# Column norms of two weight matrices: the four blocks of squares are added on VectorE before TensorE sums over partitions

## The chip, the core and the metric

The kernel runs on one core of a Trainium2 chip. The metric is the device time of one execution in microseconds (us); lower is better. A core has five engines that run side by side, each through its own list of instructions in order: TensorE (PE: matrix products, with PEld for the loading of the stationary operand), VectorE (DVE), ScalarE (ACT), GpSimd (POOL) and SyncE (SP, which here only starts DMAs). They wait for one another by semaphores. An instruction that waits holds up all that stands behind it on its engine.

## What is computed

An attention over a small memory of 32 slots per head, followed by a two-layer network on its output. Cut to what matters:

```
a = softmax of phi over the 576 positions
k_m, v_m = a^T k, a^T v                       # 32 x 64 per head
attn = softmax(q k_m^T / 8)
x = attn v_m                                  # 4608 tokens x 512
h = x @ w_in                                  # w_in 512 x 2048
out = (h - tanh(h)) @ w_out                   # w_out 2048 x 512
```

The kernel has a quick path that is exact enough only while the numbers stay within bounds (h small, weights neither tiny nor large). So it also computes, beside the main work, the sums of squares of the weights' columns and compares them with a lower and an upper bound. Should a comparison fail, a second, slower path (`wide_path`) runs after the first.

## The kernel before

The weights are split into a high and a low float16 part, `win_hi` and `win_lo`, `wout_hi` and `wout_lo`. The tokens go in 18 units `u` of 256, and each unit in four blocks `fb` of 512 hidden features. After a start whose order is written out by hand, a loop walks over *slots*, one `(u, fb)` each, numbered from 18; a slot takes about 8 us. Every engine then follows the order in which the program emits instructions (`in_order`), and no scheduler moves anything.

One slot emits, in this order:

- `mm1`: 24 or more matrix products of TensorE into the tile `hs` (L534), and ScalarE's square of `hs` (L541);
- `g1`, VectorE (L549), and then the words of the first part of the slot's plan;
- ScalarE's second square (L554); `a_forms`, four float16 sums or differences of VectorE into `f` (L581); and `g2`, VectorE (L558);
- `mm2_blocks`: the second product for a slot further back, L660 and L667 on TensorE;
- the words of the second part of the plan (behind `;`);
- `g2_high`, ScalarE (L563), and `g3`, GpSimd (L568);
- late steps, such as the squares of the weights (`SI`, `SO`) and GpSimd's pass over reloaded weights (`CW`, tile `fy`, L408); then `evict`, which on the last block of a unit sends the finished output through VectorE (L716 to L727);
- the words of the third part (behind `|`); after that the next slot's `mm1`.

The squares: `squares_in(fb)` takes 512 columns of `win_hi` in four blocks of 128 rows and leaves `sqi`, a tile of 128 partitions x (4 x 512) float16; `squares_out(part)` does the same for `wout_hi` into `sqo`. One slot later `norms_in` and `norms_out` sum them over the partitions. For each group of 128 columns TensorE loads a 128x128 block of squares as its stationary operand and multiplies it by a column of ones; the four blocks are accumulated in PSUM. That is 16 pairs of load and product in each of eight places, the slots 32, 40, 48, 55, 57, 59, 61 and 63 (`NI0` to `NI3`, `NO0` to `NO3`). They stand between a slot's `mm2_blocks` and the next slot's `mm1`. ScalarE copies the four resulting columns out (L428, L445).

Of the kernel before, what the change touches and what calls it, by code (L numbers as in the profile page):

```python
# [14 lines left out]
ALU = mybir.AluOpType  # L15
# [3 lines left out]
P = 128  # L19
# [20 lines left out]
CW = (  # L40
    0.33333331252017, -0.13333128520786, 0.053934788850892, -0.021660115374759,
    0.0082189218977914, -0.0025104593252184, 0.000420695493864,
)
# [1 line left out]


V_WIN = (2.0 ** -12, 0.0025)
WI_WIN = (2.0 ** -6, 1.5)
WO_WIN = (2.0 ** -6, 3.5)
N_F1 = 32  # L50


# [254 lines left out]
def split_path(ctx, tc, c, ins, out):  # L307
    nc = tc.nc
# [53 lines left out]
    def conv(p):  # L362

        ts = [big.tile([P, 512], U32, tag=W_TAG[p], name=f"wt{p}{i}") for i in range(2)]
        yield from to_f32(p, ts)
        yield
        tfs[p] = [t.bitcast(F32) for t in ts]
        his[p] = half_of(p, win_hi, wout_hi)
        for i in range(2):
            nc.scalar.activation(his[p][:, i], tfs[p][i], AF.Copy, scale=S_W)  # L370
# [9 lines left out]
    def low(p):  # L380
        lo = low_of(p)
        for i in range(2):
            nc.vector.scalar_tensor_tensor(
                lo[:, i], tfs[p][i], S_W, his[p][:, i], op0=ALU.mult, op1=ALU.subtract
            )

    def low_pe(p):
        lo = low_of(p)
        pw = ps_h.tile([P, 2, 512], F32, tag="h", name=f"pw{p}")
        for i in range(2):  # L390
            nc.tensor.matmul(pw[:, i], c["idw"], tfs[p][i], start=True, stop=False)
            nc.tensor.matmul(pw[:, i], c["nid16"], his[p][:, i], start=False, stop=True)
        yield
        nc.scalar.activation(lo, pw, AF.Copy)

    def low_pool(p):
        lo = low_of(p)
        for i in range(2):
            nc.scalar.activation(tfs[p][i], tfs[p][i], AF.Copy, scale=S_W)
        yield  # L400
        for i in range(2):
            nc.gpsimd.tensor_tensor(lo[:, i], tfs[p][i], his[p][:, i], op=ALU.subtract)
# [11 lines left out]
    def squares_in(fb):  # L414
        acc["q", fb] = big.tile([P, 4, 512], F16, tag="q" if fb < 3 else "e", name=f"sqi{fb}", bufs=2 if fb < 3 else 1)
        nc.scalar.activation(acc["q", fb], win_hi[:, :, 512 * fb : 512 * fb + 512], AF.Square, scale=S_Q)

    def norms_in(fb):
        sq = acc.pop(("q", fb))
        pa = ps_a.tile([P, 2, 512], F32, tag="pa", name=f"pni{fb}")  # L420
        for k in range(4):
            for pr in range(4):
                nc.tensor.matmul(
                    pa[:, 0, k : k + 1], sq[:, pr, P * k : P * k + P], c["ones16"],
                    start=(pr == 0), stop=(pr == 3),
                )
        o = N_F1 + 2 * B + 4 * fb
        nc.scalar.activation(stat[:, o : o + 4], pa[:, 0, 0:4], AF.Copy, scale=(S_W * S_Q) ** -2)  # L428

# [4 lines left out]
    def norms_out(part):  # L434
        if part == 0:
            acc["n"] = big.tile([P, 4, 4], F32, tag="wn", name="wn", bufs=1)
        sq = acc.pop(("q", part))
        pa = ps_a.tile([P, 2, 512], F32, tag="pa", name=f"pno{part}")
        for k in range(4):
            for i in range(4):  # L440
                nc.tensor.matmul(
                    pa[:, 0, k : k + 1], sq[:, i, P * k : P * k + P], c["ones16"],
                    start=(i == 0), stop=(i == 3),
                )
        nc.scalar.activation(acc["n"][:, :, part], pa[:, 0, 0:4], AF.Copy, scale=(S_W * S_Q) ** -2)  # L445
        if part == 3:
            o = N_CHECK - 4
            nc.vector.tensor_reduce(stat[:, o : o + 4], acc["n"], axis=AX.X, op=ALU.add)
# [146 lines left out]
    acc = {}  # L595
# [149 lines left out]
    def two(f, g, *x):  # L745
# [15 lines left out]
        "AT": lambda b, t: att.soft_turn(b, st[b], t), "AS": lambda b, t: att_split(b, t, nc.gpsimd), "ASv": lambda b, t: att_split(b, t, nc.vector),  # L761
        "Z": warm, "P": att_p, "PL": att_pl, "H": mm1, "a": lambda u, fb: two(g1, g1_square, u, fb), "b": lambda u, fb: two(g2, g2_high, u, fb), "c": lambda u, fb: g3(u, fb, nc.gpsimd), "cv": lambda u, fb: g3(u, fb, nc.vector), "PLp": att_pl_pe,
        "T": lambda x, y: conv(10 * x + y), "L": lambda x, y: low_pool(10 * x + y), "Lv": lambda x, y: low(10 * x + y), "Lp": lambda x, y: low_pe(10 * x + y),
        "G": b_form, "SI": squares_in, "NI": norms_in, "SO": squares_out, "NO": norms_out,
        "GG": lambda: check(tc, c, big), "GX": lambda: check_all(tc, c, ps_a),
        "M": lambda u, fb: mm2(u, fb, fb in (0, 2), fb in (1, 3)), "R": load_part, "OP": save_part, "O": save,
    }
# [15 lines left out]
    for word in START.split():  # L783
        if ":" in word:
            k, tag = word.split(":")
# [15 lines left out]
    )  # L801

    PLAN_C = (
# [5 lines left out]
    )  # L809
    tasks = {}  # L810
# [82 lines left out]
def check(tc, c, big):  # L893
    nc = tc.nc
    stat = c["stat"]
    good = big.tile([P, N_CHECK], F32, tag="good", name="good", bufs=1)
    nc.vector.tensor_scalar(good[:, 0:N_F1], stat[:, 0:N_F1], 0.0, None, op0=ALU.is_le)
    o = N_F1
    for n, (lo, hi) in ((2 * B, V_WIN), (DF // P, WI_WIN), (DM // P, WO_WIN)):
        s, g = stat[:, o : o + n], good[:, o : o + n]  # L900
        nc.vector.tensor_scalar(g, s, lo, None, op0=ALU.is_ge)
        nc.vector.scalar_tensor_tensor(g, s, hi, g, op0=ALU.is_le, op1=ALU.mult)
        o += n
    row = big.tile([P, 1], F32, tag="grow", name="grow", bufs=1)
    nc.vector.tensor_reduce(row, good, axis=AX.X, op=ALU.add)
    c["row"] = row


def check_all(tc, c, ps_a):
    nc = tc.nc  # L910
    pa = ps_a.tile([P, 2, 512], F32, tag="pa", name="pgood")
    nc.tensor.matmul(pa[:, 0, 0:1], c["ones"], c["row"], start=True, stop=True)
    nc.vector.tensor_scalar(c["bad"], pa[:, 0, 0:1], P * N_CHECK - 0.5, None, op0=ALU.is_lt)
# [120 lines left out]
@with_exitstack  # L1034
def tile_kernel(ctx: ExitStack, tc: tile.TileContext, qt, kva, kvt, pha, phx, w_in, w_out, out):
    nc = tc.nc
    ins = dict(qt=qt, kva=kva, kvt=kvt, pha=pha, phx=phx, w_in=w_in, w_out=w_out)
    const = ctx.enter_context(tc.tile_pool(name="const", bufs=1))
    c = {}
    for name, shape, dt in (  # L1040
        ("ident", [P, P], F32), ("ones", [P, P], F32), ("ones16", [P, 1], F16), ("one", [P, 1], F32),
        ("beta", [P, 1], F32), ("idw", [P, P], F32), ("nidp", [P, P], F16), ("idw", [P, P], F32), ("nid16", [P, P], F16), ("stat", [P, N_CHECK], F32), ("bad", [P, 1], I32),
    ):
        c[name] = const.tile(shape, dt, name=name)
    make_identity(nc, c["ident"])
    nc.vector.tensor_scalar(c["nid16"], c["ident"], -1.0, None, op0=ALU.mult)
    nc.vector.tensor_scalar(c["nidp"], c["ident"], -S_V * S_W / S_P, None, op0=ALU.mult)
    nc.vector.tensor_scalar(c["idw"], c["ident"], S_W, None, op0=ALU.mult)
    nc.gpsimd.memset(c["ones"], 1.0)
    nc.gpsimd.memset(c["ones16"], 1.0)  # L1050
    nc.gpsimd.memset(c["one"], 1.0)
    nc.gpsimd.memset(c["beta"], BETA)
    with ExitStack() as inner:
        split_path(inner, tc, c, ins, out)
    bad = nc.values_load(c["bad"][0:1, 0:1], min_val=0, max_val=1)
    with tc.If(bad > 0):
        with ExitStack() as inner:
            wide_path(inner, tc, c, ins, out)
# [39 lines left out]
```

## Time and profile before

| | |
|---|---|
| runs shown | 678.45, 680.75 and 677.93 us; median 678.45 us |
| the profiled execution | 678.71 us, of which 676.9 us are the span of the profile |
| mean granted TensorE clock | 0.986 of full speed |
| HBM traffic | 73.55 MB read, 11.53 MB written |

A line of the timeline gives the start in us from the span's start, the duration in us, the engine, the line of the program, the operation, what is written and read, and its shape; `x16` means that 16 such instructions were merged. What stands in square brackets is the idle time of the engine ahead of the instruction, and what ended it. A line on the instructions of one tile or one source line gives smallest, median and largest duration in ns instead.

### The profile page before, as it was taken

The numbers are of one execution on the slowest core, as the hardware profiler recorded it, in microseconds if no ns is written. First come the engines' busy times: TensorE is split into PE (matmuls) and PEld (weight loads), VectorE is DVE, ScalarE is ACT, GpSimd is POOL, SyncE is SP. The second block draws the span as 40 slices with busy tenths as digits, with TensorE's granted clock in tenths as the row PEclk, the third lists the DMA queues.
The fourth block names the chain that finished last, engine by engine and source line by source line (L and its number), as shares of the span: only waits on it lengthen the run. The fifth ranks groups of instructions, "written<-read, shape, count | busy, mean of one in ns | idle before, by whom it ended". The sixth has DMA issues, their size and how long they took to land.

```text
span 676.9 us, 15461 instructions
## 1 busy us (share of the span) xinstructions
PE 645.2 (95%) x6628; PEld 449.3 (66%) x6628; DVE 512.3 (76%) x799; ACT 376.0 (56%) x506; POOL 256.7 (38%) x170
## 2 busy tenths in 40 slices
PE   4678989999999999999999999999999999999996
PEld 1335465565646567787777777777777777887874
DVE  4599899989655677966697868886888586867573
ACT  2458477765543356554566455646555587766541
POOL 0032623423211334452345344534453555455521
PEclk9878999999999999999999999999999999999999
DMA  8679653422312142125331523152415233234201
GB/s 346 248 270 386 242 172 128 177 99 80 125 64 90 54 148 72 63 52 188 92 112 45 191 73 128 48 192 68 133 49 183 68 103 126 72 120 132 84 32 37
DMA packets 26428, 86.16 MB, mean 127 GB/s; under 512 B 2928, under 2 KB 3184, under 8 KB 25584
## 3 DMA queue, kind: packets, MB, share of 16 engines
q1 hardware_dynamic: 25056, 82.87, 35.5%
q10 hardware_dynamic: 1296, 2.23, 0.9%
q8 instruction: 54, 0.88, 0.5%
q14 instruction: 22, 0.18, 0.1%
HBM read 73.55 MB, written 11.53 MB: 126 GB/s over the span
## 4 chain that ended last, share of the span: by engine, by line
PE 69%; DVE 6%; ACT 1%; DMA 1%; issue 0%; SPq 0%; DVEq 0%; ACTq 0%
PE hs L534 19%; PE o L660 12%; PE x L667 12%; PE o L667 9%; PE o L611 7%; PE h L534 2%; PE pp L486 2%; PE pkv L196 2%; DVE f L581 2%; PE o1h L611 2%; DVE h L549 1%; DVE h L558 1%; PE psc L240 1%; DMA kv<-in_kva_dram 1%; ACT u L541 1%
## 5 line engine op out<-in xcount | busy, mean ns | idle before, releaser
L568 POOL TENSOR_TENSOR g<-h,g 128x1024 f16<-128x1024 f32 x64 | 145.2, 2269 | 322.1 <-ACT g L563 212.3
L534 PEld LDWEIGHTS <-ph 128*128 128x128 f16 x2304 | 177.5, 98 | 22.4 <-issue 6.4
L534 PE MATMUL hs<-ah,ph 128*128 128x256 f16 (+3 forms) x1088 | 145.8, 248 | 0.0
L549 DVE SCALAR_TENSOR_TENSOR h<-hs,u 128x1024 f32<-128x1024 f32 x52 | 63.5, 1221 | 97.0 <-ACT u L541 93.8
L563 ACT ACTIVATE g<-h 128x1024 f16<-128x1024 f32 x72 | 76.0, 1055 | 94.8 <-DVE h L558 86.0
L534 PE MATMUL hs<-al,ph 128*128 128x256 f16 (+3 forms) x544 | 122.1, 248 | 0.0
L554 ACT ACTIVATE u<-u,beta 128x1024 f32<-128x1024 f32 x72 | 82.6, 1148 | 62.6 <-DVE h L549 62.1
L660 PE MATMUL o<-wout_hi,g 128*128 128x512 f16 x416 | 100.6, 380 | 1.5 <-DVE r L727 1.5
L558 DVE SCALAR_TENSOR_TENSOR h<-u,h 128x1024 f32<-128x1024 f32 x72 | 88.9, 1234 | 5.0 <-ACT u L554 4.6
L667 PEld LDWEIGHTS <-f 128*128 128x128 f16 x832 | 81.4, 98 | 9.5
L611 PEld LDWEIGHTS <-g 128*128 128x128 f16 x480 | 45.8, 98 | 59.0 <-issue 4.5
L541 ACT ACTIVATE u<-hs 128x1024 f32<-128x1024 f32 x52 | 53.0, 1020 | 52.5 <-PE hs L534 52.4
L611 PE MATMUL o<-wout_hi,g 128*128 128x512 f16 x256 | 78.5, 379 | 1.1 <-ACT g L563 0.6
L667 PE MATMUL x<-bt,f 128*128 128x256 f16 x624 | 76.6, 273 | 0.0
L667 PEld LDWEIGHTS <-g 128*128 128x128 f16 x624 | 60.6, 98 | 21.6 <-issue 0.8
L660 PEld LDWEIGHTS <-g 128*128 128x128 f16 x416 | 38.5, 98 | 48.4 <-issue 13.4
L581 DVE TENSOR_TENSOR f<-g 128x512 f16<-128x512 f16 x104 | 58.3, 600 | 3.4 <-POOL g L568 3.4
L534 PE MATMUL h<-ah,ph 128*128 128x256 f16 (+2 forms) x448 | 57.1, 245 | 0.0
L534 PE MATMUL h<-al,ph 128*128 128x256 f16 (+2 forms) x224 | 48.6, 245 | 0.6 <-DVE al L477 0.6
L611 PE MATMUL o<-wout_lo,g 128*128 128x512 f16 x128 | 48.5, 379 | 0.0
L504 DVE SCALAR_TENSOR_TENSOR ph<-pp,ph 128x1024 f16<-128x1024 f32 x30 | 36.4, 1213 | 1.9 <-ACT ph L499 1.7
L499 ACT ACTIVATE ph<-pp 128x1024 f16<-128x1024 f32 x32 | 32.5, 1016 | 4.3 <-PE pp L486 4.3
(137 smaller groups left out, 954.4 us busy)
## 6 DMA issues: line engine op xcount, KB each, us to landing
kv<-in_kva_dram SPq DMA_DIRECT2D x20, 516.0 KB, 4.0
q<-in_qt_dram SPq DMA_DIRECT2D x16, 576.0 KB, 4.1
chk<-in_w_in_dram SPq DMA_DIRECT2D x16, 512.0 KB, 5.1
chk<-in_w_out_dram SPq DMA_DIRECT2D x16, 512.0 KB, 3.5
out_dram<-r SPq DMA_DIRECT2D x25, 256.0 KB, 2.5
kv<-in_kva_dram SPq DMA_DIRECT2D x6, 1032.0 KB, 9.7
raws<-in_w_in_dram SPq DMA_DIRECT2D x12, 512.0 KB, 6.0
raw<-in_w_out_dram SPq DMA_DIRECT2D x12, 512.0 KB, 6.2
```

Of the source, the lines that this page charges most:

```text
L504: nc.vector.scalar_tensor_tensor(pl, pa, S_P / (S_V * S_W), ph, op0=ALU.mult, op1=ALU.subtract)
L534: nc.tensor.matmul(hp[:, k, tu : tu + w], px[:, g, cs], d[ax][:, g, ta : ta + w], start=(n == 0), stop=(n == 5),)
L541: nc.scalar.activation(uu, hp, AF.Square, scale=1.0 / (S_A * S_P))
L549: nc.vector.scalar_tensor_tensor(h3, hp, C2 * S_G / (S_A * S_P), uu, op0=ALU.mult, op1=ALU.mult)
L554: nc.scalar.activation(uu, uu, AF.Square, bias=c["beta"])
L558: nc.vector.scalar_tensor_tensor(h3, uu, CC, h3, op0=ALU.add, op1=ALU.mult)
L563: nc.scalar.activation(gg[:, 0], h3, AF.Copy)
L568: eng.tensor_tensor(gg[:, 1], h3, gg[:, 0], op=ALU.subtract)
L581: nc.vector.tensor_tensor(o, x, y, op=op)
L611: nc.tensor.matmul(o, gx[:, k, P * tt : P * tt + P], wx[:, 4 * fb + k, :], start=(first and k == 0 and wx is wout_hi and gx is gh), stop=( ...
L660: nc.tensor.matmul(o[th], gg[:, 0, k, P * th : P * th + P], wout_hi[:, 4 * fb + k, :], start=(first and k == 0), stop=False)
L667: nc.tensor.matmul(dst, a(1 - n, kk), b(n, kk), start=(new and kk == 0 and n == 0), stop=(end and kk == 1 and n == 1))
```

## The change

VectorE adds the four blocks of squares in place, in two steps: blocks 0 and 1 plus blocks 2 and 3 (128x1024), then block 0 plus block 1 (128x512). TensorE then makes one pair of load and product for each group of 128 columns, 4 in place of 16. The new step, `SS`, stands in the second part of the plan of the same slot as the norms. The bounds of the comparison are drawn in by 0.2% for the rounding of the added float16 sums.

```
-WI_WIN = (2.0 ** -6, 1.5)
-WO_WIN = (2.0 ** -6, 3.5)
+WI_WIN = (1.002 * 2.0 ** -6, 1.497)
+WO_WIN = (1.002 * 2.0 ** -6, 3.493)
...
+    def squares_sum(i):
+        sq = acc["q", i]
+        nc.vector.tensor_tensor(sq[:, 0:2], sq[:, 0:2], sq[:, 2:4], op=ALU.add)
+        nc.vector.tensor_tensor(sq[:, 0], sq[:, 0], sq[:, 1], op=ALU.add)
...
         for k in range(4):
-            for pr in range(4):
-                nc.tensor.matmul(
-                    pa[:, 0, k : k + 1], sq[:, pr, P * k : P * k + P], c["ones16"],
-                    start=(pr == 0), stop=(pr == 3),
-                )
+            nc.tensor.matmul(pa[:, 0, k : k + 1], sq[:, 0, P * k : P * k + P], c["ones16"], start=True, stop=True)
...
-    (31, "CW CE SI0"), (32, "CW CW | NI0"),
+    (31, "CW CE SI0"), (32, "CW CW ; SS0 | NI0"),
...
-    (56, "CW CW CQ CQ SO0"), (57, "CW CW CQ CQ | NO0"),
+    (56, "CW CW CQ CQ SO0"), (57, "CW CW CQ CQ ; SS0 | NO0"),
```

`norms_out` is changed as `norms_in` is, and the other six places of the plan get `SS` in the same way.

Where the new instructions stand on their engines is shown at two places. The first is slot 32. This is VectorE there before the change: `f` are the sums of `a_forms`, `h` is `g2`, `sz` belongs to the attention's second softmax, and the next `h` is `g1` of slot 33.

```order
L581 TENSOR_TENSOR f_4010<-g_3958,f_4010 128x2x256
L558 SCALAR_TENSOR_TENSOR h_3996<-u_3994,h_3996 128x1024
L280 TENSOR_REDUCE sz_4061<-sc_3910 128x18
L281 TENSOR_SCALAR sz_4061<-sz_4061 128x18
L282 RECIPROCAL sz_4061<-sz_4061 128x18
L549 SCALAR_TENSOR_TENSOR h_4110<-hs,u_4108 128x1024
```

And this is VectorE at the same place now (lines below the edit are two less).

```order
L579 TENSOR_TENSOR f_4010<-g_3958,f_4010 128x2x256
L556 SCALAR_TENSOR_TENSOR h_3996<-u_3994,h_3996 128x1024
L421 TENSOR_TENSOR sqi_3965<-sqi_3965 128x1024
L422 TENSOR_TENSOR sqi_3965<-sqi_3965 128x512
L280 TENSOR_REDUCE sz_4063<-sc_3910 128x18
L281 TENSOR_SCALAR sz_4063<-sz_4063 128x18
L282 RECIPROCAL sz_4063<-sz_4063 128x18
L547 SCALAR_TENSOR_TENSOR h_4100<-hs,u_4098 128x1024
```

The two sums stand right behind `g2` (L556), ahead of the attention's work. On TensorE the place of the norms is unchanged, behind the last product of `mm2_blocks` (`f` as stationary operand) and ahead of the next slot's `mm1` (`hs`). So it stands there now, with the semaphores that are waited for:

```order
L665 LDWEIGHTS f_3916
L665 MATMUL o_3813<-wout_lo,f_3916 128x256
L428 LDWEIGHTS sqi_3965 [waits DVE_49,Activation_49]
L428 MATMUL pni_4068<-ones_60,sqi_3965 128x1 [waits PE_49]
L428 LDWEIGHTS sqi_3965
L428 MATMUL pni_4068<-ones_60,sqi_3965 128x1
L428 LDWEIGHTS sqi_3965
L428 MATMUL pni_4068<-ones_60,sqi_3965 128x1
L428 LDWEIGHTS sqi_3965
L428 MATMUL pni_4068<-ones_60,sqi_3965 128x1
L532 LDWEIGHTS ph_2992
L532 MATMUL hs<-ah_3041,ph_2992 128x256
```

Before, 16 such pairs (L423) stood in the place of these four. The first load now has to wait for VectorE's second sum; the `mm1` of the next slot (`hs`, L532) stands behind it.

The second place is slot 57, the last block of a unit, where the output leaves through VectorE. Before, the rows `r` of `evict` followed `g2` at once:

```order
L558 SCALAR_TENSOR_TENSOR h_7052<-u_7050,h_7052 128x1024
L716 SCALAR_TENSOR_TENSOR r_7061<-x,r_7061 128x256
L717 SCALAR_TENSOR_TENSOR r_7062<-x,r_7061 128x256
L718 TENSOR_TENSOR r_7061<-r_7061,r_7062 128x256
L719 TENSOR_TENSOR r_7062<-r_7062 128x256
L727 SCALAR_TENSOR_TENSOR r_7061<-o_6717,r_7061 128x512
```

Now the two sums stand between them:

```order
L556 SCALAR_TENSOR_TENSOR h_7012<-u_7010,h_7012 128x1024
L421 TENSOR_TENSOR sqo_6979<-sqo_6979 128x1024
L422 TENSOR_TENSOR sqo_6979<-sqo_6979 128x512
L714 SCALAR_TENSOR_TENSOR r_7021<-x,r_7021 128x256
L715 SCALAR_TENSOR_TENSOR r_7022<-x,r_7021 128x256
L716 TENSOR_TENSOR r_7021<-r_7021,r_7022 128x256
L717 TENSOR_TENSOR r_7022<-r_7022 128x256
L725 SCALAR_TENSOR_TENSOR r_7021<-o_6687,r_7021 128x512
```

All of `evict` has moved behind the sums; the same holds in slot 61. ScalarE, GpSimd and SyncE keep their order everywhere.

More of the change, by code (lines that the diff above doesn't have):

```diff
@@ L439, in norms_out @@
         for k in range(4):
[L440 to L444, printed above, removed]
+            nc.tensor.matmul(pa[:, 0, k : k + 1], sq[:, 0, P * k : P * k + P], c["ones16"], start=True, stop=True)
         nc.scalar.activation(acc["n"][:, :, part], pa[:, 0, 0:4], AF.Copy, scale=(S_W * S_Q) ** -2)
@@ L763, in split_path @@
         "T": lambda x, y: conv(10 * x + y), "L": lambda x, y: low_pool(10 * x + y), "Lv": lambda x, y: low(10 * x + y), "Lp": lambda x, y: low_pe(10 * x + y),
-        "G": b_form, "SI": squares_in, "NI": norms_in, "SO": squares_out, "NO": norms_out,
+        "G": b_form, "SI": squares_in, "NI": norms_in, "SO": squares_out, "NO": norms_out, "SS": squares_sum,
         "GG": lambda: check(tc, c, big), "GX": lambda: check_all(tc, c, ps_a),
```

8 rows, old and new, of the table PLAN_C are left out of this document.

## The prediction

> **What bounds the kernel now.** I read the page's busy shares and its chain first, then who TensorE waits for in the second half of the span, and last the timeline around the eight places where the norms are summed.
>
> ```profile
> PE 645.2 (95%) x6628; PEld 449.3 (66%) x6628; DVE 512.3 (76%) x799; ACT 376.0 (56%) x506; POOL 256.7 (38%) x170
> ...
> PE 69%; DVE 6%; ACT 1%; DMA 1%; issue 0%; SPq 0%; DVEq 0%; ACTq 0%
> ```
>
> The chain that ended last is TensorE's by 69% of the span. All eight places lie after 320 us; among TensorE's waits from 320 to 660 us the largest group is this (us in total, times, longest):
>
> ```profile
> PE o L660 <- DVE r L727: 1.5, 4, 1.0
> ```
>
> So in that stretch TensorE hardly ever waits, and a us taken from or added to its own list moves the end by a us. VectorE, busy 76% of the span, has room on average. But an average doesn't say when it has room, so the question is what VectorE is doing when TensorE arrives at the norms. This is the first place (slot 32), in the timeline:
>
> ```profile
> 334.52 1.22 DVE L558 SCALAR_TENSOR_TENSOR h<-u,h 128x1024 f32<-128x1024 f32 x1
> ...
> 335.07 0.56 PEld L423 LDWEIGHTS <-sqi 128*128 128x128 f16 x16
> 335.18 0.54 PE L423 MATMUL pni<-ones,sqi 128*128 128x1 f16 x16
> ...
> 335.58 0.27 PE L534 MATMUL hs<-ah,ph 128*128 128x256 f16 x1
> 335.66 0.74 DVE L280 TENSOR_REDUCE sz<-sc 128x18 f32<-128x576 f32 x1
> 335.77 1.06 ACT L563 ACTIVATE g<-h 128x1024 f16<-128x1024 f32 x1 [0.90 <-DVE h L558]
> ```
>
> TensorE arrives at 335.07, while VectorE is still in `g2` (L558, from 334.52). In the changed order the sums stand behind `g2`. TensorE will get there first.
>
> **What is removed.** The 16 pairs start at 335.18 and the next slot's `mm1` at 335.58: 0.40 us for 16, 25 ns a pair, although the duration shown for one product is 163 ns or so; products overlap. Twelve pairs fewer are 0.30 us per place, and 8 x 0.30 = 2.40 us in all. That is the whole gain there can be, 0.35%. The rows lie on TensorE's own list, so it is a real gain, if nothing waits.
>
> **What is added: two sums on VectorE.** No row has a 128x1024 sum of float16. The nearest are these:
>
> ```profile
> L581 DVE TENSOR_TENSOR f<-g x104: 379/417/1621, 240.9 to 665.5; 128x512 f16<-128x512 f16 x104
> ```
>
> ```profile
> L718 DVE TENSOR_TENSOR r<-r,r x13: 412/415/417, 277.4 to 669.7; 128x256 f32<-128x256 f32 x13
> ```
>
> The small sum (128x512) has its own row: 0.42 us. For the large one the floor is the same 0.42, the ceiling twice that, 0.84. A sum of 512 float16 takes as long as one of 256 float32, so an element costs half as much. A float32 pass of 1024 takes 1.22 us (L558) and one of 512 takes 0.64 (L727 below, 1.28 for two): 0.58 for 512 more, so 0.29 for 512 more of float16, and 0.42 + 0.29 = 0.71 us. I take 0.71.
>
> The next VectorE instruction starts 1.14 us after `g2` does (335.66 - 334.52). ScalarE, which waits for `g2`, starts 0.03 after its end (335.77 against 335.74); I take 0.03 for each hand-over. The second sum is then done, and TensorE let go, at the start of `g2` + 1.14 + 0.71 + 0.03 + 0.42 + 0.03 = **+2.33 us**. GpSimd could disturb this only if it were at work then; its `g3` waits for L563, which ends at 1.25 + 1.06 = 2.31 after that start, so the sums just escape it.
>
> **What TensorE waits.** At the first place 334.52 + 2.33 = 336.85 against 335.07: 1.78 us. Here are the others; the second is like the first and the third, so the third stands for both.
>
> ```profile
> 472.68 1.22 DVE L558 SCALAR_TENSOR_TENSOR h<-u,h 128x1024 f32<-128x1024 f32 x1
> 473.23 0.56 PEld L423 LDWEIGHTS <-sqi 128*128 128x128 f16 x16
> ...
> 533.60 1.22 DVE L558 SCALAR_TENSOR_TENSOR h<-u,h 128x1024 f32<-128x1024 f32 x1
> ...
> 535.04 0.56 PEld L423 LDWEIGHTS <-sqi 128*128 128x128 f16 x16
> ...
> 551.00 0.56 PEld L441 LDWEIGHTS <-sqo 128*128 128x128 f16 x16
> ...
> 551.67 1.22 DVE L558 SCALAR_TENSOR_TENSOR h<-u,h 128x1024 f32<-128x1024 f32 x1
> ...
> 567.96 0.56 PEld L441 LDWEIGHTS <-sqo 128*128 128x128 f16 x16
> ...
> 568.82 1.22 DVE L558 SCALAR_TENSOR_TENSOR h<-u,h 128x1024 f32<-128x1024 f32 x1
> ...
> 584.17 0.56 PEld L441 LDWEIGHTS <-sqo 128*128 128x128 f16 x16
> ...
> 584.85 1.22 DVE L558 SCALAR_TENSOR_TENSOR h<-u,h 128x1024 f32<-128x1024 f32 x1
> ...
> 600.38 0.56 PEld L441 LDWEIGHTS <-sqo 128*128 128x128 f16 x16
> ...
> 600.70 1.22 DVE L558 SCALAR_TENSOR_TENSOR h<-u,h 128x1024 f32<-128x1024 f32 x1
> ```
>
> From the fifth place on TensorE arrives before `g2` has even begun. By the same arithmetic (start of L558 + 2.33 - arrival) the eight waits are 1.78, 1.78, 1.78, 0.89, 3.00, 3.19, 3.01 and 2.65, together **18.1 us**. Less the 2.4 us of removed pairs, that is **+15.7 us**.
>
> What is queued behind: the whole `mm1` of the next slot, and with it that slot's chain (square on ScalarE, `g1`, second square, `g2`, `g3`). All of it hangs on `mm1` and is late by the same amount, so `g2` is no nearer to TensorE's arrival at the next place: the waits add up. Nothing later takes them up, as TensorE's own list has next to no idle time there (the 1.5 us row). The loads on SyncE's queue keep their order and get more time.
>
> **A second wait behind the first.** In slots 57 and 61 `evict` now stands behind the sums. These are the rows of slot 57:
>
> ```profile
> 547.35 2.04 POOL L408 TENSOR_TENSOR fy<-chk 128x512 f32<-128x512 f32 x2
> ...
> 549.01 1.95 DVE L581 TENSOR_TENSOR f<-g 128x512 f16<-128x512 f16 x2
> ...
> 549.34 1.34 POOL L284 TENSOR_TENSOR sc<-sc,sz 128x576 f32<-128x576 f32 x1
> ...
> 553.60 0.41 DVE L718 TENSOR_TENSOR r<-r,r 128x256 f32<-128x256 f32 x1
> ...
> 554.06 2.29 POOL L568 TENSOR_TENSOR g<-h,g 128x1024 f16<-128x1024 f32 x1 [3.38 <-ACT wn L445]
> ...
> 554.27 1.28 DVE L727 SCALAR_TENSOR_TENSOR r<-o,r 128x512 f32<-128x512 f32 x2
> ...
> 555.00 1.89 PE L660 MATMUL o<-wout_hi,g 128*128 128x512 f16 x8
> ...
> 556.32 2.03 POOL L408 TENSOR_TENSOR fy<-chk 128x512 f32<-128x512 f32 x2
> ```
>
> Two `f` sums that meet GpSimd take 1.95 us where two alone take some 0.8: they end at 550.96, 0.28 after GpSimd's L284, so each seems to wait out one GpSimd instruction. Today L718 and L719 are nearly through when GpSimd's `g3` starts at 554.06. With `evict` about 1.09 us later (0.74 for the first sum and its hand-over, 0.35 for the second), L718 comes at 554.69, in the middle of `g3`, which needs until some 556.2. If L718 waits for that, and L719 for the `fy` pass behind it (1.02 us), L719 ends near 557.9 and the first L727 at 558.55. TensorE, 2.70 us late by then (3.00 - 0.30), comes to L660 at 557.70 and needs the buffer `o` that L727 frees: 0.85 us more. If L719 slips in ahead of `fy`, it is 0. I take 0.85, as the `f` rows show one wait for each, and the same for slot 61: **+1.7 us**.
>
> **Sum.** 15.7 + 1.7 = 17.4 us on the profiled execution's 678.71 us (the median of the runs shown is 0.26 lower): **696.0 us**, 2.6% slower.
>
> **Rivals.**
>
> *The clock falls in the long waits.* The trace shows that the granted clock drops to half after pauses of TensorE:
>
> ```profile
> 28.59 1.09 PE L196 MATMUL pkv<-kv,e 128*32 128x129 f32 x32 [3.02 <-ACT e L180]
> ...
> 62.08 0.66 PE L225 MATMUL ptr<-ident,kvn 128*64 128x128 f32 x8 [1.27 <-DVE kvn L204]
> 63.74 1.00 PE L240 MATMUL psc<-q,kT 64*32 64x288 f32 x16 [1.00 <-ACT kT L232]
> ```
>
> ```profile
> 29.50:30.00 0.50, 0.50 (x20) 0.18 (x12) 0.00 (x0) 0.00 (x0) 0.00 (x0) 0.91 0.00 0
> ...
> 64.00:64.50 0.50, 0.50 (x16) 0.00 (x0) 0.50 (x1) 0.50 (x1) 0.00 (x0) 0.54 1.00 412
> 67.00:67.50 0.50, 0.50 (x4) 0.38 (x3) 0.50 (x2) 0.32 (x1) 0.10 (x1) 0.54 1.02 424
> ```
>
> The third number from the right is the granted clock. A mean of 0.91 in half a us puts the first fall at 29.91, 0.54 puts the second at 64.04, and the rise at 67.46. From fall to rise are 3.42 us, from fall to fall 34.13, ten times 3.41. So the clock seems to be set every 3.41 us by what the last 3.41 us held; these held 2.1 us of pause (26.50 to 28.59) and 2.27 (1.27 + 1.00). As the product ahead of a wait still runs for some 0.2 us into it (0.27 for one at L534), the last four waits leave the array idle for about 2.5 to 3.0 us, the first three for only 1.6. Where the steps of 3.41 us fall is chance; one holds 2.1 us of a pause of length s with a chance of (3.41 + s - 4.2)/3.41, 0.5 to 0.65 for each of the last four. That gives two or three falls of 1.7 us (3.41 at half speed): 700 us, at most 702.8 with four. Against it: the short work beside those two pauses was of float32 products that fill a part of the array, while here dense float16 products surround the pause, so the bar may lie higher. [...]
>
> *The sums are hidden.* If they were done by the time TensorE arrives, only the 2.4 us would be left: 676.3 us, not slower. That decides itself at start of `g2` + 2.33 against arrival; today's rows miss it by 0.9 to 3.2 us at all eight places. It would need VectorE to run the sums ahead of `g2`, and the order printed for the change puts them behind.
>
> *A shorter wait.* With 0.42 us for the large sum, no `evict` collision, and the 1.5 us of existing waits at L660 taken up: 15.7 - 8 x 0.29 - 1.5 = 11.9, 690.6 us. At the other end, 0.84 us (+1.0) and 0.2 us per place for waking TensorE (+1.6) give 698.6 with a held clock.
>
> *The bounds.* Narrower bounds could send the kernel into its second path only if a column's sum of squares left them; `w_in` has 512 rows of variance 1/512, `w_out` 2048 of 1/2048, so the sums lie around 1. I leave this out.
>
> **How the numbers follow.** Forecast, waits with a held clock, 693 to 698.6 us: 0.52. Clock falls as well, 698 to 703 us: 0.34. Shorter waits, 684 to 693: 0.09. Hidden: 0.05. The range runs from 691.0 to 702.5. A difference of 0.5% (3.4 us) is about what a measurement can tell from none: faster by more than that 0.01, within it 0.05, slower 0.94.
>
> **What would show each step.** On TensorE an idle stretch ahead of the norms, ended by the second sum, at all eight places, near 1.8 us three times, then 0.9, then 2.6 to 3.2 four times; the next `mm1` shifted by each wait less 0.30. The large sum near 0.71 us. In slots 57 and 61 L718 and L719 longer than 1 us and a wait of TensorE at L660. Half-clock stretches after 550 us would speak for the first rival. I am wrong at the root if VectorE's sums start before TensorE gets there, or if TensorE's list goes on past the waiting load.

## The result and the profile after

| | before | after |
|---|---|---|
| median of 6 runs | 678.34 us (677.93 to 680.75) | 696.31 us (693.15 to 698.79) |
| the profiled execution | 678.71 us, span 676.9 | 698.79 us, span 697.0 |
| mean granted TensorE clock in it | 0.986 | 0.980 |

The changed kernel is slower: 1.0261 times the time before, with a 95% interval from 1.0245 to 1.0277, or 18.0 us between the medians. The profiled execution is the longest of the six, 2.5 us over their median; its rows show more loss than a usual run has.

These are the busy times and the chain that ended last, from the page of the changed kernel:

```profile
PE 651.0 (93%) x6532; PEld 450.5 (65%) x6532; DVE 522.7 (75%) x815; ACT 376.2 (54%) x506; POOL 255.4 (37%) x170
...
PE 33%; DVE 10%; ACT 6%; issue 2%; DMA 1%; POOL 0%; SPq 0%; DVEq 0%; ACTq 0%
```

TensorE has 96 matrix products fewer and is yet busy 5.8 us longer (651.0 against 645.2): part of its work ran at a lower clock (0.81 to 0.83 of full speed in the four windows below). Of the chain only 33% is TensorE's now, against 69%; VectorE and ScalarE have entered it.

These are the rows that name the norms, from who waits for whom between 320 and 690 us (us in total, times, longest), with the row on L658, which was L660 before. The weight load (PEld) is listed apart from the product, whose rows are left out here but for one:

```profile
PEld L442 <- ACT g L561: 11.0, 4, 3.1
...
PEld L428 <- ACT g L561: 5.6, 3, 1.9
...
PE pni L428 <- DVE sqi L422: 0.6, 1, 0.6
...
PE o L658 <- DVE r L725: 0.2, 1, 0.2
```

The norms wait at all eight places. Seven of these waits are put down to ScalarE's `g` (L561), as the load waits for a semaphore of ScalarE too. The timeline of the changed kernel tells whether it is `g`. First slot 32, then the fourth place, slot 55:

```profile
334.22 1.22 DVE L556 SCALAR_TENSOR_TENSOR h<-u,h 128x1024 f32<-128x1024 f32 x1
335.35 0.69 DVE L421 TENSOR_TENSOR sqi<-sqi 128x1024 f16<-128x1024 f16 x1
335.47 1.06 ACT L561 ACTIVATE g<-h 128x1024 f16<-128x1024 f32 x1 [0.90 <-DVE h L556]
336.07 0.43 DVE L422 TENSOR_TENSOR sqi<-sqi 128x512 f16<-128x512 f16 x1
...
336.61 0.18 PEld L428 LDWEIGHTS <-sqi 128*128 128x128 f16 x4 [1.86 <-ACT g L561]
336.64 0.24 PE L428 MATMUL pni<-ones,sqi 128*128 128x1 f16 x4 [1.61 <-ACT g L561]
...
539.43 1.06 ACT L561 ACTIVATE g<-h 128x1024 f16<-128x1024 f32 x1 [2.24 <-DVE h L556]
...
539.97 0.43 DVE L422 TENSOR_TENSOR sqi<-sqi 128x512 f16<-128x512 f16 x1
...
540.45 0.17 PEld L428 LDWEIGHTS <-sqi 128*128 128x128 f16 x4 [0.90 <-DVE sqi L422]
```

In slot 32 `g` ends at 336.53 and the second sum at 336.50, so the list can't tell them apart. In slot 55 `g` ends at 540.49, after the load has started at 540.45, and the sum at 540.40. So it is the sum that lets TensorE go. In the kernel with the sums ahead of `g2`, below, the load of slot 32 starts at 333.47 us and `g` at 335.23, so the load doesn't need `g`. In the changed kernel's slot 32 the load starts 2.39 us after `g2`.

The loss is best laid out as a shift: the start of `g2` in a slot, counted from that of slot 30, less the same in the kernel before. The rows of `g2` in the timelines give it (us; the norms stand at the end of slots 32, 40, 48, 55, 57, 59, 61 and 63):

| shift at slot | 34 | 42 | 50 | 57 | 58 | 60 | 62 | 64 | 71 |
|---|---|---|---|---|---|---|---|---|---|
| the change | 1.23 | 2.47 | 4.49 | 5.32 | 9.17 | 12.94 | 17.26 | 20.25 | 20.39 |

There are three steps of 1.2, with 0.8 more at slot 46 and 0.3 at slot 54, ahead of which TensorE waits for a late load (`kv`), a step of 0.5 at the fourth place, and then four of 3 to 4.3 us. The last four are larger than the waits shown for them. These windows of the changed kernel hold the stretch behind each of the last four waits (PE busy, PEld, DVE, ACT, POOL, granted clock, DMA share, GB/s):

```profile
555.00:564.00 9.00, 6.17 (x52) 4.07 (x58) 8.76 (x12) 3.70 (x10) 5.18 (x4) 0.81 0.35 119
575.00:585.00 10.00, 7.49 (x100) 6.57 (x98) 5.48 (x9) 3.35 (x7) 4.75 (x4) 0.83 0.24 63
596.00:605.00 9.00, 6.79 (x88) 5.43 (x86) 8.57 (x13) 3.83 (x8) 3.48 (x3) 0.81 0.30 77
616.00:625.00 9.00, 6.54 (x46) 4.75 (x45) 4.03 (x8) 3.05 (x6) 4.44 (x4) 0.81 0.26 76
```

A mean clock of 0.81 over 9 us is 3.42 us at half speed, of 0.83 over 10 us 3.4. So the clock fell at each of the last four waits, near its end or just behind it (0.10 us ahead of the end to 0.91 us behind it). Last, the rows of slot 57, where `evict` meets GpSimd:

```profile
558.55 0.43 DVE L422 TENSOR_TENSOR sqo<-sqo 128x512 f16<-128x512 f16 x1
...
559.08 2.12 POOL L566 TENSOR_TENSOR g<-h,g 128x1024 f16<-128x1024 f32 x1 [3.38 <-ACT g L561]
...
559.12 0.24 PE L442 MATMUL pno<-ones,sqo 128*128 128x1 f16 x4 [2.83 <-ACT g L561]
...
559.68 1.80 DVE L716 TENSOR_TENSOR r<-r,r 128x256 f32<-128x256 f32 x1
...
561.16 2.40 POOL L408 TENSOR_TENSOR fy<-chk 128x512 f32<-128x512 f32 x2
...
561.41 1.26 DVE L717 TENSOR_TENSOR r<-r 128x256 f32<-128x256 f32 x1
```

L716 took 1.80 us where its twin took 0.41 before, and ends 0.28 after GpSimd's `g3`; L717 about 0.3 after the first of the two `fy` passes (half of 2.40). The collision is there, as forecast. But TensorE comes to L658 so late, by its own wait and the half clock, that it doesn't wait there at all in slots 58 and 62. The 0.2 us of the list lie in slot 66, behind the last place. There the kernel before has the longest of its four waits at this product; first its row, then that of the changed kernel:

```profile
619.51 1.89 PE L660 MATMUL o<-wout_hi,g 128*128 128x512 f16 x8 [1.04 <-DVE r L727]
```

```profile
639.60 1.89 PE L658 MATMUL o<-wout_hi,g 128*128 128x512 f16 x8 [0.17 <-DVE r L725]
```

The other three, of 0.17 us in slots 34, 42 and 50, are gone. So of the 1.5 us that TensorE waited there before, some 1.4 are gone.

### The profile page after: what moved, and what is told of

Read it like the earlier page. It is cut to its first block, busy times and chain, and to the rows that moved or that the text cites. A ratio compares the mean times of both kernels' runs of the same rounds, so it can differ in the third digit from the quotient of the medians.

```text
span 697.0 us, 15297 instructions
## 1 busy us (share of the span) xinstructions
PE 651.0 (93%) x6532; PEld 450.5 (65%) x6532; DVE 522.7 (75%) x815; ACT 376.2 (54%) x506; POOL 255.4 (37%) x170
## 4 chain that ended last, share of the span: by engine, by line
PE 33%; DVE 10%; ACT 6%; issue 2%; DMA 1%; POOL 0%; SPq 0%; DVEq 0%; ACTq 0%
PE hs L532 13%; PE o L658 6%; PE x L665 6%; PE o L665 5%; DVE f L579 3%; DVE h L556 3%; ACT u L539 2%; DVE h L547 2%; ACT g L561 2%; PE pp L484 1%; PE pkv L196 1%; DVE ph L502 1%; DMA kv<-in_kva_dram 1%; ACT sqo L434 1%; ACT sqi L416 1%
## 5 line engine op out<-in xcount | busy, mean ns | idle before, releaser
L532 PEld LDWEIGHTS <-ph 128*128 128x128 f16 x2304 | 181.9, 100 | 24.4 <-issue 6.2
L532 PE MATMUL hs<-ah,ph 128*128 128x256 f16 (+3 forms) x1088 | 152.2, 254 | 0.0
L532 PE MATMUL hs<-al,ph 128*128 128x256 f16 (+3 forms) x544 | 126.1, 254 | 0.0
L561 ACT ACTIVATE g<-h 128x1024 f16<-128x1024 f32 x72 | 75.9, 1055 | 89.3 <-DVE h L556 80.5
L658 PE MATMUL o<-wout_hi,g 128*128 128x512 f16 x416 | 100.7, 380 | 0.2 <-DVE r L725 0.2
L539 ACT ACTIVATE u<-hs 128x1024 f32<-128x1024 f32 x52 | 53.0, 1019 | 75.8 <-PE hs L532 75.8
L556 DVE SCALAR_TENSOR_TENSOR h<-u,h 128x1024 f32<-128x1024 f32 x72 | 89.0, 1236 | 5.0 <-ACT u L552 4.6
L658 PEld LDWEIGHTS <-g 128*128 128x128 f16 x416 | 38.3, 98 | 47.2 <-issue 12.6
L532 PE MATMUL h<-ah,ph 128*128 128x256 f16 (+2 forms) x448 | 57.4, 246 | 0.0
L579 DVE TENSOR_TENSOR f<-g 128x512 f16<-128x512 f16 x104 | 51.0, 531 | 3.4 <-POOL g L566 3.4
L532 PE MATMUL h<-al,ph 128*128 128x256 f16 (+2 forms) x224 | 48.8, 246 | 0.6 <-DVE al L475 0.6
```

The lines of the kernel that those rows point to most:

```text
L532: nc.tensor.matmul(hp[:, k, tu : tu + w], px[:, g, cs], d[ax][:, g, ta : ta + w], start=(n == 0), stop=(n == 5),)
L539: nc.scalar.activation(uu, hp, AF.Square, scale=1.0 / (S_A * S_P))
L556: nc.vector.scalar_tensor_tensor(h3, uu, CC, h3, op0=ALU.add, op1=ALU.mult)
L561: nc.scalar.activation(gg[:, 0], h3, AF.Copy)
L579: nc.vector.tensor_tensor(o, x, y, op=op)
L658: nc.tensor.matmul(o[th], gg[:, 0, k, P * th : P * th + P], wout_hi[:, 4 * fb + k, :], start=(first and k == 0), stop=False)
```

## The experiments

All plans quoted are those of slots 32, 40, 48 and so on; one place stands for those that are edited alike. Each median is against the kernel before on the same chip (678.51, 678.39 and 678.50 us in three groups of runs).

### Norms one slot later

The sums stay where the change put them; the norms move into the second part of the next slot, so that TensorE has no reason to wait.

```
-(32, "CW CW ; SS0 | NI0"),
+(32, "CW CW ; SS0"), (33, "; NI0"),
...
-(57, "CW CW CQ CQ ; SS0 | NO0"), (58, "CW CQ SO1"),
+(57, "CW CW CQ CQ ; SS0"), (58, "CW CQ SO1 ; NO0"),
```

> The sums stay where the change has them; only the norms' four pairs move, from the end of the same slot to the second part of the next slot, behind its mm2_blocks. If TensorE's waits for the sums are the cause, all eight are gone and with them the falls of the clock: 678.3 - 2.4 = 676 us, give or take the 1.7 of the evict collision, which is still there and can now show itself at L658 because TensorE is no longer late (up to 3.5 us at each of two places): 676 to 683. If the sums themselves are the cause (VectorE late with g1, f and g2 for whoever needs them), nothing changes: 693 to 699.

Measured: 687.30 us (686.50 to 688.17), ratio 1.0135 [1.0119, 1.0150]. The waits at the norms are gone, and about half of the loss with them. Up to slot 57 nothing is left of it: the shift is -0.01 at slot 42, 0.25 at slot 50 and 0.01 at slot 57. Then it grows to 2.80, 4.16, 7.43 and 8.78 at slots 58, 60, 62 and 64. So VectorE's sums are free of charge in slots 32, 40, 48 and 55, and dear in 57 and 61, the last blocks of two units. Slot 57 in the timeline of this run shows why:

```profile
552.94 0.43 DVE L422 TENSOR_TENSOR sqo<-sqo 128x512 f16<-128x512 f16 x1
...
553.47 2.12 POOL L566 TENSOR_TENSOR g<-h,g 128x1024 f16<-128x1024 f32 x1 [3.38 <-ACT g L561]
...
554.07 1.80 DVE L716 TENSOR_TENSOR r<-r,r 128x256 f32<-128x256 f32 x1
...
555.55 2.40 POOL L408 TENSOR_TENSOR fy<-chk 128x512 f32<-128x512 f32 x2
555.80 1.25 DVE L717 TENSOR_TENSOR r<-r 128x256 f32<-128x256 f32 x1
556.98 1.27 DVE L725 SCALAR_TENSOR_TENSOR r<-o,r 128x512 f32<-128x512 f32 x2
557.71 3.07 PE L658 MATMUL o<-wout_hi,g 128*128 128x512 f16 x8 [3.72 <-DVE r L725]
```

The sums push `evict` into GpSimd's `g3` and `fy`, L716 and L717 wait one instruction out each, and TensorE, now on time, waits 3.72 us for the buffer `o` at L658. Behind that wait the clock falls too: in the windows of this run its mean is 0.72 from 557 to 563 us, 3.4 us at half speed, which answers for the 1.36 us between slots 58 and 60.

### Sums ahead of `g2`

The sums move from the second part of the plan to the first, where the squares are long ready.

```
-(32, "CW CW ; SS0 | NI0"),
+(32, "CW CW SS0 | NI0"),
```

> The norms stay where the change has them; the sums move from the second part of the slot to the first, behind g1 and ahead of the f sums and g2. Waits theory: from the rows of before, the sums are done at 334.2 against an arrival at 335.07 in the first place, so no wait in the first four; in the last four they meet GpSimd and end 0 to 0.6 us after TensorE arrives: 676 to 678. evict isn't behind them any more, so no collision there. Sums theory: as much work on VectorE, in front of g2, so at least as slow as the change: 696 or more.

Measured: 687.25 us (685.13 to 688.40), ratio 1.0141 [1.0125, 1.0156]. The shift is 1.06 us at slot 32 already, which is 0.65 + 0.42, the length of the two sums. After that it is 0.91, 1.81 and 3.20 at slots 34, 42 and 50, 4.81 at slot 57 and 7.93 at the end: about 1 us per place in nearly all of them. So VectorE has no room ahead of `g2` either. The waits of TensorE that stand for it (320 to 690 us):

```profile
PE o L658 <- DVE r L725: 6.5, 4, 2.4
PE pp L484 <- ACT wn L443: 2.2, 3, 0.8
PE pno L442 <- DVE sqo L422: 1.5, 2, 1.1
```

Most of it comes back at L658: TensorE waits there for `evict`, which ends VectorE's chain of the unit, 6.5 us where the kernel before has 1.5.

### No sums

The four pairs without the sums; a quarter of the squares goes into the norms.

```
-(32, "CW CW ; SS0 | NI0"),
+(32, "CW CW | NI0"),
```

> The two sums are left out, so the norms hold a quarter of the squares; TensorE makes its four pairs at once. This measures the gain of the removed pairs alone: 8 x 0.30 = 2.4 us, 676.0 us, if they lie on the path; 678.3 if they were hidden.

Measured: 678.65 us (677.57 to 680.48), ratio 1.0008 [0.9997, 1.0019]. The 96 removed pairs are worth nothing by themselves, where 2.4 us less (0.9965) had been counted. The shift is 0.00 at slots 34 and 42, so not even the first place gains its 0.30 us. From slot 50 on it is between 0.42 and 0.70, from a late load. The waits show where the time went:

```profile
PE o L658 <- DVE r L725: 2.7, 4, 1.3
...
PE pp L484 <- ACT wn L443: 0.4, 2, 0.2
```

These were 1.5 us at L660 (L658 here) and no such wait at L484: TensorE is sooner and waits the more. One by one, the waits at L658 are 0.46 us in slots 34, 42 and 50, where they were 0.17, and 1.34 in slot 66, where it was 1.04. So at four of the eight places all of the 0.30 us is lost in this wait. In slots 58 and 60 TensorE waits 0.2 us at L484 for ScalarE's copy of the norms, which stands behind `g` and so behind `g2`. The two places that are left, slots 55 and 61, were not followed.

### Sums beside the norms

The sums go into blocks 2 and 3, which nobody reads; TensorE makes its 16 pairs on blocks 0 and 1, each twice, and doesn't wait. Blocks 2 and 3 are left out of the norms.

```
-        nc.vector.tensor_tensor(sq[:, 0:2], sq[:, 0:2], sq[:, 2:4], op=ALU.add)
-        nc.vector.tensor_tensor(sq[:, 0], sq[:, 0], sq[:, 1], op=ALU.add)
+        nc.vector.tensor_tensor(sq[:, 2:4], sq[:, 0:2], sq[:, 2:4], op=ALU.add)
+        nc.vector.tensor_tensor(sq[:, 2], sq[:, 2], sq[:, 3], op=ALU.add)
...
+                    pa[:, 0, k : k + 1], sq[:, pr % 2, P * k : P * k + P], c["ones16"],
```

> The sums are made at the same place and of the same size, but into blocks 2 and 3, and TensorE makes 16 pairs from blocks 0 and 1 (each twice), so it doesn't wait for VectorE; blocks 2 and 3 are left out of the norms. This is the sums' own cost. If VectorE has room and evict escapes GpSimd: 678.3. If evict is caught as the prediction has it, L725 ends 3.5 us after TensorE needs it in two slots: about 685, with TensorE waiting at the first product of the next unit and nowhere else.

Measured: 688.06 us (686.90 to 689.53), ratio 1.0148 [1.0130, 1.0165]. This is the load on VectorE alone, and it behaves as the norms one slot later did: the shift is -0.02 at slot 50, 0.59 at 57, then 3.39, 4.92, 8.18 and 9.55 at 58, 60, 62 and 64. Two kernels that differ in the number of pairs and in their place agree, so the loss in slots 57 and 61 belongs to the sums ahead of `evict`.

### The waits filled with products

The change as it is, with 11 to 13 matrix products of 128x512 ahead of each of the last four norms, into a part of the norms' buffer that nobody reads. TensorE works through its waits; the sums and `evict` stand as in the change.

```
+        for _ in range((12, 13, 12, 11)[part]):
+            nc.tensor.matmul(
+                pa[:, 1], c["nid16"], c["nid16"].unsqueeze(1).to_broadcast((P, 4, P)), start=True, stop=True
+            )
```

> [...] Clock theory: no half clock after 550 us, and 4.4 us (what the change's places 5 to 8 lost beyond their waits) are back, less what the evict collision then shows at L658, up to 0.85 in each of two slots: 693 to 695 us, with a smaller spread than the change's 693.2 to 698.8. If the half clock costs nothing on the path: 696.3, as the change.

Measured: 693.91 us (691.96 to 695.47), ratio 1.0207 [1.0185, 1.0230]. One window over the last five places, in this run and then in the changed kernel:

```profile
540.00:640.00 100.00, 98.04 (x943) 72.51 (x941) 72.17 (x111) 62.00 (x89) 48.45 (x34) 1.00 0.29 92
```

```profile
540.00:640.00 100.00, 89.36 (x854) 68.26 (x855) 67.68 (x104) 58.88 (x85) 45.30 (x32) 0.93 0.28 90
```

The products took 216 ns each (in slot 59, 13 of them from 577.76 us to the norms at 580.57). The clock is held at 1.00 against 0.93. The shift from slot 57 to 71 is 15.13 - 5.27 = 9.9 us against 20.39 - 5.32 = 15.1, so the half clock cost 5.2 us in the profiled executions, net of what TensorE now waits for `evict`:

```profile
PE o L662 <- DVE r L729: 1.0, 3, 0.6
```

These three waits (L662 is L658 of the changed kernel) are 0.55 us in slot 58, 0.26 in slot 62 and 0.17 in slot 66.

Between the medians the half clock cost 696.31 - 693.91 = 2.4 us. The other runs of the changed kernel have granted clocks of 0.981 to 0.989, and the one at 0.989 took 693.15 us. Both speak for fewer than four falls in the usual run, but only the profiled one shows where its clock fell. With the clock held, 15.5 us of loss remain (693.91 - 678.39).

### The change for `w_in` alone

Sums and four pairs at the first four places, 16 pairs as before at the last four.

```
-(57, "CW CW CQ CQ ; SS0 | NO0"),
+(57, "CW CW CQ CQ | NO0"),
```

> The change for w_in alone (slots 32, 40, 48, 55); w_out keeps its 16 pairs and no sums. From the change's own trace these four places lost 1.24 three times and 0.50: 678.4 + 4.2 = 682.6 us, and no half clock after 300 us. If the first four waits are too short to count, 678.4.

Measured: 683.60 us (682.57 to 684.46), ratio 1.0068 [1.0044, 1.0092]. The shift is that of the change up to slot 57 (1.23, 2.46, 4.42, 4.94) and stays at 4.94 from there. What is lost at one place is neither made up nor added to later, so the places can be added up.

### Sums moved out of the units' last slots

Norms one slot later, and the squares of `w_out` one slot later as well, so that their sums fall into slots 58, 60, 62 and 64, away from `evict`. In the second kernel one of GpSimd's two `fy` passes of slots 32, 40 and 48 also moves a slot ahead.

```
-(56, "CW CW CQ CQ SO0"), (57, "CW CW CQ CQ ; SS0 | NO0"), (58, "CW CQ SO1"),
+(56, "CW CW CQ CQ ; NI3"), (57, "CW CW CQ CQ SO0"), (58, "CW CQ ; SS0"),
...
-(31, "CW CE SI0"), (32, "CW CW ; SS0 | NI0"),
+(31, "CW CW CE SI0"), (32, "CW ; SS0"), (33, "; NI0"),
```

> As e1 (norms one slot after the sums), and the squares of w_out one slot later, so that their sums stand in slots 58, 60, 62 and 64 in place of 57, 59, 61 and 63: no sum stands ahead of an evict any more. If the 9 us of e1 came from evict behind the sums, they are gone, and what is left is the removed pairs' gain, which e3 found to be nothing: 677.5 to 679. If VectorE's 8.8 us of sums cost by themselves, 685 or more.

> As e6, and in slots 32, 40 and 48 one of GpSimd's two passes over reloaded weights (fy) is moved one slot earlier, so that the f sums of the unit's last slot (33, 41, 49) meet one GpSimd instruction less and evict ends earlier. If the removed pairs' gain is lost because L658 waits for evict in slots 34, 42 and 50, those waits (0.17 us, and 0.47 without sums) go: 0.4 to 0.5 us at each of three places, 676.5 to 677.5. If something else holds TensorE there, as e6.

Measured: 682.13 us (680.95 to 684.09), ratio 1.0053 [1.0032, 1.0074], and 681.67 us (679.92 to 683.93), ratio 1.0041 [1.0025, 1.0056]. Both miss. In the first one the first four places cost nothing (shift 0.04 at slot 50, -0.20 at 57), but `w_out` still does: the shift is 0.58, -0.12, 0.64, 0.65, 1.88 and 2.02 at slots 58, 59, 60, 61, 62 and 64. The steps lie at the ends of slots 57, 59 and 61, where the squares now stand; the first of them is regained a slot later. Here are ScalarE's rows at the end of slot 59, of the kernel before and then of this one:

```profile
571.04 0.16 ACT L445 ACTIVATE wn<-pno 128x4 f32<-128x4 f32 x1
...
571.41 1.02 ACT L541 ACTIVATE u<-hs 128x1024 f32<-128x1024 f32 x1 [0.21 <-PE hs L534]
```

```profile
570.55 1.89 ACT L434 ACTIVATE sqo<-wout_hi 128x2048 f16<-128x2048 f16 x1
...
572.35 1.00 ACT L539 ACTIVATE u<-hs 128x1024 f32<-128x1024 f32 x1
```

The weights' square (L434, until 572.44) stands ahead of the square of `hs` (L539), which starts right behind it, 4.01 us after its slot's `g2` (568.34) where it was 2.59 (571.41 - 568.82). So ScalarE has no room there for 1.9 us, as VectorE has none ahead of `evict`. Why the delay of slot 58 is regained and the two others are not was not tried apart. In the second kernel the first three places even gain some: -0.27 at slot 34, -0.54 at 42.

### What is left to win

Two kernels take the parts that gained or were free. One has sums and four pairs for `w_in` alone, with the norms one slot later and the `fy` passes moved. The other is the kernel before, with the three `fy` passes moved and nothing else:

```
-(31, "CW CE SI0"), (32, "CW CW | NI0"),
+(31, "CW CW CE SI0"), (32, "CW | NI0"),
```

> The best of the parts: sums and four pairs for w_in alone, the norms one slot after the sums, one fy pass of slots 32, 40 and 48 a slot earlier; w_out as before the change. e8's trace lost nothing and gained some 0.3 us at each of the first three places and 0.2 at the fourth. If those gains reach the end: 678.4 - 1.1 = 677.3 us. If a later wait takes them back, as it took back those of e3: 678.4.

> The kernel before the change with nothing but the three fy passes moved one slot earlier; no sums, 16 pairs everywhere. The waits of 0.17 us at L660 in slots 34, 42 and 50 should go: 678.4 - 0.5 = 677.9 us. If e9 gains over this one, the removed pairs are worth something once evict is out of the way: up to 0.3 us at each of four places, 1.2 us. If not, they are worth nothing on this path.

Measured: 678.30 us (676.60 to 679.38), ratio 0.9996 [0.9986, 1.0005], for the first, and 677.14 us (675.98 to 678.97), ratio 0.9983 [0.9973, 0.9993], for the second. The second is the fastest of all, by 1.2 us, and has no sums. At slot 57 the shift is -0.40 and -0.68. The first meets a late load near slot 46; at slot 42, ahead of it, the two stand at -0.51 and -0.46. So the pairs that the first removes gain next to nothing even with `fy` out of the way, where 0.60 us for two places had been counted. The traces show why: without the pairs TensorE waits 0.21 us at that product for `evict` in each of slots 34, 42 and 50, and with them not at all. These are the kernel before and then the second one, in slots 33 and 34 (its times are 1.13 us less throughout, as its slot 30 began so much sooner):

```profile
339.05 2.04 POOL L408 TENSOR_TENSOR fy<-chk 128x512 f32<-128x512 f32 x2
...
340.66 2.01 DVE L581 TENSOR_TENSOR f<-g 128x512 f16<-128x512 f16 x2
...
346.71 1.89 PE L660 MATMUL o<-wout_hi,g 128*128 128x512 f16 x8 [0.17 <-DVE r L727]
```

```profile
338.50 1.04 POOL L408 TENSOR_TENSOR fy<-chk 128x512 f32<-128x512 f32 x1
...
339.53 1.75 DVE L581 TENSOR_TENSOR f<-g 128x512 f16<-128x512 f16 x2
...
345.34 1.90 PE L660 MATMUL o<-wout_hi,g 128*128 128x512 f16 x8
```

With one `fy` pass where two had been, VectorE's two `f` sums take 1.75 us and not 2.01, `evict` ends so much sooner, and the wait of 0.17 us at L660 is gone. That is the 0.23 us per place by which the shift falls (-0.23, -0.46, -0.67 at slots 34, 42 and 50).

## Why the prediction was right, and where its steps were off

*TensorE gets to the norms first, and waits for the second sum.* Right, at all eight places. The large sum was put at 0.71 us and took 0.69, the small one 0.42 and 0.43; TensorE's load starts 2.39 us after `g2` where 2.33 had been worked out. The loads' waits are 5.6 us in the first three places (forecast 3 x 1.78 = 5.3), 0.90 in the fourth (0.89) and 11.0 in the last four (3.00 + 3.19 + 3.01 + 2.65 = 11.9): 17.5 against 18.1 us. The 0.2 us that the upper bound allows for waking TensorE is shown by no run; the load starts 0.11 us after the second sum's end in slot 32 and 0.05 in slot 55.

*"The waits add up", "Nothing later takes them up".* The first is right: with the change at the first four places alone the shift stays at 4.94 us to the end. The second is not quite. The prediction put the 1.5 us row at next to nothing, and some 1.4 us of it are taken up by the new delay: 0.17 us in each of slots 34, 42 and 50, which is most of why the first three places cost 1.24 us each where 1.48 had been forecast, and 0.87 in slot 66.

*"It is a real gain, if nothing waits": 2.40 us for 96 pairs.* Wrong as a gain by itself. It ran on TensorE's list, and that list was the bound by the chain and by the small row of waits. But VectorE's chain, with `evict` at its end, already came 0.17 us later than TensorE to the end of such a unit (the wait at L660 in slot 34); with TensorE 0.30 sooner the wait is 0.46. Without the sums the gain is 0 (1.0008). Inside the change it counts, as there the wait, not `evict`, decides when the next `mm1` starts, and 4 pairs behind a wait are sooner done than 16 (0.13 us from the first load to `mm1` in slot 32, where it was 0.51). The rival that hides the sums drew on the same gain: 676.3 us. With the sums hidden from TensorE the kernel took 687.3.

*VectorE "has room on average" and the question is when.* The prediction asked it only for the moment at which TensorE arrives. The runs answer it for the rest of the slot. Behind `g2` in slots 32, 40, 48 and 55 the sums are free. Ahead of `g2` they cost their own length, about 1 us per place. Ahead of `evict` they cost about 3 us in each of the slots 57 and 61, and the clock's fall on top.

*The second wait, +1.7 us.* The mechanism was right (L716 1.80 us, L717 1.26), the term too large. With the clock held it is 0.55 us in slot 58 and 0.26 in slot 62. In slot 58 the first row of `evict` that frees `o` ends 6.5 us after the `g2` of slot 57, where 6.9 had been worked out. In the changed kernel nothing is left of it, as the half clock holds TensorE's `mm1` back until `evict` is done.

*The clock.* The forecast had it held, with a chance of 0.34 against it, two or three falls of 1.7 us. That it holds through pauses of 2.5 to 3.0 us was the author's estimate and is shown by no run: in the profiled execution it fell four times, at pauses of 2.83, 2.51, 2.21 and 2.46 us, for 5.2 us, and the medians differ by 2.4. The sum came out within 0.3 us of the median because two errors cancel, and that closeness is luck: with a held clock the loss is 15.5 us and not 17.4, and the clock adds 2.4. By its route, then, the result lies between the forecast and its first rival. The profiled execution with the clock held (15.1 us) shows the terms: 0.7 us less in the first three places, 0.9 less for the second wait, 0.9 taken up in slot 66, 0.8 less at the norms of slots 59 and 61 (read from the starts of `mm1`), and 1.0 more for a late load.

*A shorter wait, 690.6 us.* It did not happen in the waits at the norms, but its idea that the waits at L660 would be taken up was right for 1.4 of the 1.5 us.

What stays open: a late load adds 0.3 to 0.9 us near slot 46, and up to 0.6 near slot 54, in several of the runs and not in others, and nothing was tried on it; what takes up the removed pairs at slots 55 and 61; and why the granted clock differs from run to run.

## What to carry to other kernels

Moving a sum off the bounding engine pays only if the engine that takes it over finishes before the bounding one arrives: read in the timeline what stands ahead of it in that very slot, and what stands behind it. An engine's idle share is not room; where its chain ends a unit and frees a buffer, a microsecond there cost three here, and the same microsecond in another slot cost none. Work removed from the bounding engine gains nothing when a second chain ends within a few tenths of a microsecond of it (0.17 us here, where 0.30 was removed), so look at what the shortest existing waits are for before counting a gain.

## What the runs showed of the hardware

The clock fell at pauses of 2.21 to 2.83 us, shorter than 3.41 us, the step in which it was seen to change; that step is an estimate from the times of the falls. These stretches of the changed kernel place the falls:

```profile
559.50:560.00 0.50, 0.50 (x5) 0.36 (x4) 0.50 (x2) 0.07 (x1) 0.50 (x1) 0.54 0.00 0
562.50:563.00 0.50, 0.50 (x5) 0.35 (x3) 0.50 (x2) 0.00 (x0) 0.50 (x1) 0.54 0.00 0
...
580.00:580.50 0.50, 0.38 (x6) 0.39 (x7) 0.50 (x1) 0.10 (x2) 0.36 (x1) 0.52 0.00 0
600.50:601.00 0.50, 0.50 (x11) 0.49 (x9) 0.50 (x2) 0.00 (x0) 0.50 (x1) 0.50 0.00 0
620.50:621.00 0.50, 0.50 (x7) 0.45 (x5) 0.17 (x1) 0.03 (x1) 0.50 (x1) 0.98 0.00 0
```

Between 560.0 and 562.5 us the granted clock is 0.50. A mean of 0.54 in half a us then puts the first fall at 559.54 and its end at 562.96, 3.42 us later; the next falls come at 580.02, 600.50 and 620.98, each 20.48 us on, six times 3.41. Two slots with a pause and a fall take about that long here (19.8 to 21.0 us between the last four norms), so a pause that meets a step of the clock is followed by others that meet it in much the same way; that this is why all four fell was not tested. The pauses at the four falls were 2.83, 2.51, 2.21 and 2.46 us, with dense float16 work around them; those of the first three places, 1.6 us, brought no fall (granted clock 1.00 from 300 to 540 us). The longest wait at L658 of the kernel with the sums ahead of `g2`, 2.4 us, shows none either: no step of its shift is larger than 1.06 us, where a fall of 3.4 us at half speed takes 1.7, and its mean granted clock is 0.992.

A sum on VectorE waited out a GpSimd instruction. This is the small sum in slot 58 of the kernel with the norms and the squares moved:

```profile
562.28 2.13 POOL L566 TENSOR_TENSOR g<-h,g 128x1024 f16<-128x1024 f32 x1 [4.50 <-ACT g L561]
...
562.41 2.28 DVE L422 TENSOR_TENSOR sqo<-sqo 128x512 f16<-128x512 f16 x1
```

It took 2.28 us in place of 0.43, and ended 0.28 after `g3`; L716 in slot 57 did the same (1.80 us in place of 0.41), as shown above. Why it waits is shown by no run.
